# Attention into top-1 expert layers on one Trainium2 core: rows of 528 floats in place of 576, with the partial logits copied to a tile of their own

## The chip, the core and the metric

The kernel runs on one core of one Trainium2 chip, in one launch. Its time is the device time in microseconds (us); the figure shown is the median of three runs. An "execution" below is one such run; one further execution was taken with the hardware profiler, and all rows below come from that one.

## The reference

For each of 8 batches and 8 heads, 576 tokens are compressed into 32 memory slots (a softmax of `phi` over the tokens gives the weights `a`), each query attends over those 32 slots, and the heads are put side by side as the input `x` (4608 tokens of 512) of a layer with 8 experts, of which each token uses one.

```
a = softmax(phi over seq);  k_m = a^T k;  v_m = a^T v           # 32 slots per head
x = softmax(q k_m^T / sqrt(64)) v_m                             # heads side by side: [4608, 512]
logits = x @ w_gate;  e = argmax(logits)
gate = softmax(logits)[e] * sigmoid(x @ w_output_gate)[e]
out = gate * (relu(x @ w1[e]) @ w2[e])
```

## The kernel before

Work goes by pairs of batches (`bp`, four of them, 1152 tokens each). `memories` makes the slots of a pair. `attention` runs 20 steps, five to a pair; the order of the parts inside a step is written out by hand (`ORDER`, line 37): score matmuls (`scores`, L846), transposition and subtraction of the maximum (`shift`), exponential (`expo`), division, transposition back, and then the value matmuls `values` (L892) twice for a step, for two chunks of 128 tokens (one chunk in a pair's fifth step).

The operand of the value matmuls holds, for each group of two heads, 128 columns of values and 16 more columns: the slots' values already multiplied by the two gate matrices. So for each token the product has four quarters of 144 = `XQ` floats: 128 of `x`, and 16 partial sums of the 8 logits and the 8 output-gate logits. It lies in two banks of PSUM, two quarters in each. `values` copies the whole of it, 128x576, with one instruction of ScalarE (ACT) to the tile `xo` (L904); `store` (L1008) writes `xo` to the DRAM table `xs`, whose rows are `XROW` = 576 floats, and eight parts later a reduction on VectorE (DVE, L1021) adds up the four partial sums out of `xo` into `lg`. PSUM has two buffers of such banks (one in the joint stage below); scores and values take turns in them. The tile `xo` has two buffers.

When a pair is done, `rank` (L906) picks the expert of each token and its gate, writes the gate over the 16 partial sums of each row's first quarter (`gt`, L980 to 985), and works out lists of rows by expert (`route_early`, `route_late`). The DMA queue of SyncE (SP) issues loads, stores and the gate writes in program order; GpSimd (POOL) issues the gathers. `gather` (L524) fetches 128 rows of `xs` for a tile: the first five groups as whole rows (L537), the rest as quarters of a row, one indirect DMA for each quarter (L531). `turn_x` (L1052) turns the gathered rows so that features lie on partitions, and `several` and `single` run the two expert products, with each fp32 weight split into two parts.

From step 17 of 20 on, attention is interleaved with the expert work by hooks between the matmuls (the joint stage); before that, TensorE has only attention to do.

Of the kernel before, what the change touches and what calls it, by code (L numbers as in the profile page):

```python
# [17 lines left out]
P = 128  # L18
# [39 lines left out]
LAST = 1  # L58
WHOLE = tuple(range(NPE))
XQ = 144  # L60
XROW = 4 * XQ


HEADS = (0, 2, 4, 6, 1, 3, 5, 7)
# [3 lines left out]
def attention_moe(tc, phiT, kv, qT, wgo, wall, out):  # L68
# [3 lines left out]
    with contextlib.ExitStack() as ctx:  # L72
# [451 lines left out]
        def gather(z):  # L524
            z["xg"] = xgs.tile()
            for k in range(z["nb"]):
                q = z["q0"] + k
                if z["quart"]:
                    rows = 4 * z["rows"]
                    for b in range(quarters(z, k)):  # L530
                        G.indirect_dma_start(  # L531
                            out=z["xg"][:, k, XQ * b:XQ * b + XQ], out_offset=None,
                            in_=xs[0:z["rows"]].rearrange("t (a q) -> (t a) q", a=4),
                            in_offset=bass.IndirectOffsetOnAxis(ap=z["idx"][2][:, b, q:q + 1], axis=0),
                            bounds_check=rows - 1, oob_is_err=False)
                    continue
                G.indirect_dma_start(  # L537
                    out=z["xg"][:, k], out_offset=None, in_=xs[0:z["rows"]],
                    in_offset=bass.IndirectOffsetOnAxis(ap=z["idx"][0][:, q:q + 1], axis=0),
                    bounds_check=z["rows"] - 1, oob_is_err=False)  # L540
# [348 lines left out]
            V.transpose(z["aT"][:, 0:n * M].rearrange("p (a m) -> p a m", m=M), z["ea"][:, 0:n, 0:M])  # L889
            tick()  # L890

        def values(bp, c, z, xo):  # L892

            px = banks()
            for g in range(2):
                sl = slice(XQ * g, XQ * g + XQ)
                for b in (c // 4,) if c < 8 else (0, 1):
                    o, n = (256 * g + (c % 2) * P, P) if c < 8 else (128 * g + 64 * b, 64)
                    to = 0 if c < 8 else 64 * b
                    for r in range(2):  # L900
                        h = slice(64 * r, 64 * r + 64)
                        T.matmul(px[to:to + n, r, sl], z["aT"][h, o:o + n], ves[2 * bp + b][h, g],  # L902
                                 start=True, stop=True)
            A.copy(xo[:, c % 2], px[:, :, 0:2 * XQ])  # L904

        def rank(bp, lg):  # L906

# [13 lines left out]
            rki = rt.tile([P, NCH], I32, name="rki")  # L921
            ri = rt.tile([P, NCH], I32, name="ri")
            row = rt.tile([P, NCH], F32, name="row")
            gt = rt.tile([P, NCH, XQ - P], F32, name="gt")
            oh = ohg[:, cs]
            dscb = desc[:].unsqueeze(1).to_broadcast(b3)
            lmb = lm[:].unsqueeze(2).to_broadcast(b3)
# [22 lines left out]
            def rest():  # L950
                yield from take_pr()
                yield from hold(LATE["pe"])

                pr = ps_r.tile([P, NCH, E], F32, name="pr")
                T.matmul(pr[:], strict[:], oh, start=True, stop=False)
                if bp:
                    T.matmul(pr[:], ones_b[:], ohcs[bp - 1][:].unsqueeze(1).to_broadcast(b3), start=False, stop=False)
                for c in range(1, NCH):
                    T.matmul(pr[:, c:], ones_b[:], oh[:, 0:NCH - c], start=False, stop=(c == NCH - 1))
                yield  # L960
                V.tensor_reduce(gd[:], w2_[:], axis=AX.X, op=ALU.add)
                A.activation(zs[:], zs[:], AF.Exp, scale=-1.0)
                yield
                yield from hold(LATE["dve"])
                V.tensor_tensor(w1_[:], oh, pr[:], ALU.mult)
                taken.clear()
                V.tensor_scalar(gd[:], gd[:], 1e-9, None, ALU.add)
                yield
                with nc.allow_low_precision("whole numbers"):
                    V.tensor_reduce(rki[:], w1_[:], axis=AX.X, op=ALU.add)  # L970
                V.tensor_scalar(zs[:], zs[:], 1.0, None, ALU.add)
                yield
                V.tensor_scalar(ri[:], rki[:], 127, None, ALU.bitwise_and)
                V.tensor_scalar(jg[:, cs], rki[:], 7, None, ALU.arith_shift_right)
                V.tensor_tensor(gd[:], gd[:], zs[:], ALU.mult)
                yield
                V.tensor_copy(row[:], ri[:])  # L977
                V.reciprocal(gd[:], gd[:])
                yield
                V.tensor_copy(gt[:], gd[:].unsqueeze(2).to_broadcast([P, NCH, XQ - P]))  # L980
                for b in range(2):
                    nc.sync.dma_start(
                        xs[t0 + b * S:t0 + b * S + 512, P:XQ].rearrange("(c p) d -> p c d", p=P),
                        gt[:, 4 * b:4 * b + 4])
                    nc.sync.dma_start(xs[t0 + b * S + 512:t0 + b * S + 576, P:XQ], gt[64 * b:64 * b + 64, 8])
                for c in range(NCH):
                    (G if AWP else V).tensor_scalar(  # L987
                        Aw[:, bp * NCH + c], iota_row[:], row[:, c:c + 1], None, ALU.is_equal)
                    if c % 3 == 2:
                        yield  # L990
                ranked.append(bp)
# [13 lines left out]
                        gens.remove(g)  # L1005
                yield

        def store(bp, c2, xo, lg):  # L1008
            t0 = bp * 2 * S
            b, n = c2 // 2, 2 if c2 < 4 else 1  # L1010
            if c2 < 4:
                r = t0 + b * S + (c2 % 2) * 256
                nc.sync.dma_start(xs[r:r + 256].rearrange("(c p) d -> p c d", p=P),
                                  xo[:].rearrange("p c r d -> p c (r d)"))
            else:
                for b_ in range(2):
                    nc.sync.dma_start(
                        xs[t0 + b_ * S + 512:t0 + b_ * S + 576],
                        xo[64 * b_:64 * b_ + 64, 0].rearrange("p r d -> p (r d)"))
            xl = xo[:].rearrange("p c r (g d) -> p c (r g) d", g=2)[:, 0:n, :, P:XQ]  # L1020
            defer("lg", lambda: V.tensor_reduce(  # L1021
                lg[:, 2 * c2:2 * c2 + n], xl.rearrange("p c q l -> p c l q"), axis=AX.X, op=ALU.add))

        def last(g):
            r = None
# [26 lines left out]
        def turn_x(z, c):  # L1052
# [4 lines left out]
            if c == 0:  # L1057
                z["x"] = (mo.tile([P, 4, 3 * P], F32R, name="xh"),
                          None if nb == 2 else mo.tile([P, 4, 3 * P], F32R, name="xl"))
                if z["quart"]:  # L1060
                    z["xt"] = {}
                    z["g"] = env["xt"].tile([P, 3], F32, name="gx")
                    for b in range(4):
                        k = nb - (nb == 2 and b > 1)
                        A.copy(z["g"][32 * b:32 * b + 32, 0:k], xg[0:32, 0:k, XQ * b + P])
            xh, xl = z["x"]
            if z["quart"]:

# [14 lines left out]
            else:  # L1083
# [1 line left out]
                    return  # L1085
                pt = bank([512], "ps")
                for k in range(nb):
                    T.transpose(pt[:, k * P:(k + 1) * P], xg[:, k, c * XQ:c * XQ + P], ident[:])
                pt = pt[:, 0:n]
            A.copy(xh[:, c, 0:n], pt)  # L1090
            V.tensor_tensor(xl[:, c, 0:n], pt, xh[:, c, 0:n].bitcast(F32), ALU.subtract)
# [21 lines left out]
        def attention():  # L1113
# [8 lines left out]
            for t in range(NT + LAG["V"]):  # L1122
                for w in ORDER:
# [12 lines left out]
                    elif w == "V0" and 0 <= g < NT:  # L1136
# [2 lines left out]
                            mem.step()  # L1139
                        if g == 5 * bp:  # L1140
                            lgs[bp] = rt.tile([P, NCH, 16], F32, name="lg", bufs=2)
                        xo = wk.tile([P, 2, 2, 2 * XQ], F32, name="xo", bufs=2)
                        values(bp, 2 * c, st[g], xo)
                    elif w == "V1" and 0 <= g < NT:
                        if c < 4:
                            values(bp, 2 * c + 1, st[g], xo)
                        store(bp, c, xo, lgs[bp])
                    elif w == "C" and 0 < g < NT:
                        while 2 * (g // 5) + (g % 5 >= 2) not in kTs:
                            mem.step()  # L1150
# [293 lines left out]
```

## Time and profile before

| | |
|---|---|
| median of three runs | 553.86 us (553.79 to 554.71) |
| the profiled execution | 555.65 us, its span 553.9 us |
| TensorE (PE) busy | 509.0 us (92%) |
| VectorE, ScalarE, GpSimd busy | 352.0, 287.9, 232.6 us |
| mean granted clock of TensorE | 0.969 |
| traffic | 123.54 MB, 223 GB/s over the span |

The span runs from the first to the last instruction; 1.75 us of the profiled execution lie outside it. "Granted clock" is the share of full speed that TensorE was given. Busy shares over the whole span mix an attention stage (to about 117 us), in which no engine is busy all the time, with an expert stage, in which TensorE is.

### The profile page before, as it was taken

The numbers are of one execution on the slowest core, as the hardware profiler recorded it, in microseconds if no ns is written. First come the engines' busy times: TensorE is split into PE (matmuls) and PEld (weight loads), VectorE is DVE, ScalarE is ACT, GpSimd is POOL, SyncE is SP. The second block draws the span as 40 slices with busy tenths as digits, with TensorE's granted clock in tenths as the row PEclk, the third lists the DMA queues.
The fourth block names the chain that finished last, engine by engine and source line by source line (L and its number), as shares of the span: only waits on it lengthen the run. The fifth ranks groups of instructions, "written<-read, shape, count | busy, mean of one in ns | idle before, by whom it ended". The sixth has DMA issues, their size and how long they took to land. (4 is left out here: it accounts for less than half of the span.)

```text
span 553.9 us, 10578 instructions
## 1 busy us (share of the span) xinstructions
PE 509.0 (92%) x3859; PEld 437.6 (79%) x3859; DVE 352.0 (64%) x779; ACT 287.9 (52%) x536; POOL 232.6 (42%) x254
## 2 busy tenths in 40 slices
PE   3788877599999999999999999999999999999993
PEld 2455555388689799898998989897999899888982
DVE  4384979957776659996436556944786387549310
ACT  3475765454454446553435546834775377358310
POOL 2242585851434034410466562563447463710101
PEclk9877989979999999999999999999999999999997
DMA  8999999995457756963547574875586577643001
GB/s 310 416 389 392 411 373 400 320 351 175 132 192 240 225 168 222 309 183 115 154 139 259 174 233 126 262 219 182 179 264 177 190 244 241 201 162 98 30 21 43
DMA packets 41998, 123.54 MB, mean 223 GB/s; under 512 B 10256, under 2 KB 10320, under 8 KB 41552
## 3 DMA queue, kind: packets, MB, share of 16 engines
q1 hardware_dynamic: 35136, 102.71, 56.0%
q0 software_dynamic: 6800, 20.06, 10.3%
q8 instruction: 32, 0.52, 0.4%
q14 instruction: 30, 0.25, 0.1%
HBM read 102.40 MB, written 20.35 MB: 222 GB/s over the span
## 5 line engine op out<-in xcount | busy, mean ns | idle before, releaser
L1275 PE MATMUL bps<-whl,hh 128*128 128x512 f32 x640 | 193.6, 394 | 0.9 <-issue 0.9
L1238 PE MATMUL bps<-xh,whl 128*128 128x384 f32 x640 | 166.0, 336 | 0.0
L590 DVE TENSOR_TENSOR whl<-w,whl 128x1024 fp32r<-128x1024 f32 x112 | 136.1, 1220 | 11.6 <-ACT whl L576 11.2
L1275 PEld LDWEIGHTS bps<-whl,hh 128*128 128x128 f32 x640 | 119.9, 188 | 26.5 <-issue 2.2
L576 ACT CAST whl<-w 128x1024 fp32r<-128x1024 f32 x112 | 116.4, 1044 | 19.3 <-PE bps L1275 14.9
L1238 PEld LDWEIGHTS bps<-xh,whl 128*128 128x128 f32 x640 | 115.8, 188 | 1.3 <-issue 0.6
L531 POOL DMA_INDIRECT xg<-xs,idx_ql x84 | 98.2, 1168 | 25.6 <-issue 23.8
L1238 PE MATMUL bps<-xl,whl 128*128 128x384 f32 x320 | 107.0, 334 | 0.0
L1275 PE MATMUL bps<-whl,hl 128*128 128x512 f32 x240 | 93.8, 391 | 0.5 <-issue 0.5
L1243 DVE SCALAR_TENSOR_TENSOR hl<-bps,hh 128x384 fp32r<-128x384 f32 x80 | 43.9, 554 | 69.9 <-ACT hh L1242 48.1
L1242 ACT ACTIVATE hh<-bps 128x384 fp32r<-128x384 f32 x80 | 38.9, 492 | 85.2 <-PE bps L1238 70.8
L1211 POOL DMA_INDIRECT out<-y,idx_ol x23 | 25.0, 1089 | 113.3 <-ACT y L1210 54.2
L1238 PEld LDWEIGHTS bps<-xl,whl 128*128 128x128 f32 x320 | 60.1, 188 | 0.3
L1275 PEld LDWEIGHTS bps<-whl,hl 128*128 128x128 f32 x240 | 45.1, 188 | 9.1 <-issue 0.8
L871 POOL TENSOR_TENSOR ea<-ea,mx 128x512 f32<-128x512 f32 (+1 forms) x20 | 19.3, 967 | 46.8 <-DVE mx L869 42.4
L1233 PE MATMUL bps<-xh,whl 128*128 128x384 f32 x128 | 37.7, 338 | 0.0
L1234 PE MATMUL bps<-xh,whl 128*128 128x256 f32 x128 | 35.7, 279 | 0.0
L904 ACT COPY xo<-bpd 128x576 f32<-128x576 f32 x36 | 22.6, 639 | 20.6 <-PE bpd L902 11.9
L1210 ACT ACTIVATE y<-bps,gx 128x512 f32<-128x512 f32 x19 | 13.1, 687 | 36.8 <-PE bps L1275 30.1
L1211 POOL DMA_INDIRECT out<-y,idx_ob x9 | 10.0, 1112 | 48.8 <-ACT y L1210 38.0
L902 PE MATMUL bpd<-ve_b,aT 64*128 64x144 f32 (+1 forms) x320 | 27.8, 321 | 3.0 <-DVE ea L865 3.0
L987 POOL TENSOR_SCALAR Aw<-iota_row,row 128x128 bf16<-128x128 bf16 x36 | 25.8, 735 | 8.9 <-DVE row L977 8.9
(263 smaller groups left out, 586.8 us busy)
## 6 DMA issues: line engine op xcount, KB each, us to landing
w<-wall SPq DMA_DIRECT2D x112, 512.0 KB
kvt<-kv SPq DMA_DIRECT2D x32, 512.0 KB
xs<-xo SPq DMA_DIRECT2D x16, 576.0 KB
qt<-qT SPq DMA_DIRECT2D x16, 512.0 KB
ph<-phiT SPq DMA_DIRECT2D x3, 1152.0 KB
kv<-kv SPq DMA_DIRECT2D x4, 512.0 KB
xg<-xs,idx_ql POOLq DMA_INDIRECT x84
ph<-phiT SPq DMA_DIRECT2D x4, 288.0 KB
```

The source lines that it names most:

```text
L531: G.indirect_dma_start(out=z["xg"][:, k, XQ * b:XQ * b + XQ], out_offset=None, in_=xs[0:z["rows"]].rearrange("t (a q) -> (t a) q", a=4), i ...
L576: A.copy(hl[:, 0], w[:])
L590: V.tensor_tensor(hl[:, 1], w[:], hl[:, 0].bitcast(F32), ALU.subtract)
L902: T.matmul(px[to:to + n, r, sl], z["aT"][h, o:o + n], ves[2 * bp + b][h, g], start=True, stop=True)
L987: (G if AWP else V).tensor_scalar(Aw[:, bp * NCH + c], iota_row[:], row[:, c:c + 1], None, ALU.is_equal)
L1211: G.indirect_dma_start(out=out, out_offset=bass.IndirectOffsetOnAxis(ap=z["idx"][1][0:n, z["q0"] + k:z["q0"] + k + 1], axis=0), in_=y[0:n] ...
L1233: T.matmul(pb, w[:, 0, o:o + P], x[0][:, cc], start=(cc == 0), stop=False)
L1234: T.matmul(pb[:, 0:256], w[:, 1, o:o + P], x[0][:, cc, 0:256], start=False, stop=(cc == 3))
L1238: T.matmul(pb, w[:, b, o:o + P], x[a][:, cc, 0:n_], start=(n == 0), stop=(n == 11))
L1242: A.activation(h_[:, j], pb, AF.Relu)
L1243: V.scalar_tensor_tensor(l_[:, j], pb, 0.0, h_[:, j].bitcast(F32), ALU.max, ALU.subtract)
L1275: T.matmul(py[k], a, w[:, b, DM * f:DM * f + DM], start=(u == 4 and f == 0 and n == 0), stop=(u == 7 and f == 1 and n == len(ps) - 1))
```

## The change

Rows of `xs` go from 4x144 to 4x132 floats: 128 values of each quarter and 4 more. The copy from PSUM to `xo` takes those 132 columns of each quarter (528 elements), and a second copy takes the 16 partial sums of each quarter (64 elements) to a new tile `xl` of two buffers, from which the reduction now reads. The first 4 of the 16 partial sums are still stored, and the gate is written over them (4 floats a row in place of 16). Counts of DMAs, gathers and matmuls stay.

```diff
-XROW = 4 * XQ
+XR = 132
+XROW = 4 * XR
...
                         G.indirect_dma_start(
-                            out=z["xg"][:, k, XQ * b:XQ * b + XQ], out_offset=None,
+                            out=z["xg"][:, k, XR * b:XR * b + XR], out_offset=None,
...
-        def values(bp, c, z, xo):
+        def values(bp, c, z, xo, xl):
...
-            A.copy(xo[:, c % 2], px[:, :, 0:2 * XQ])
+            pv = px[:, :, 0:2 * XQ].rearrange("p r (g d) -> p r g d", g=2)
+            A.copy(xo[:, c % 2], pv[:, :, :, 0:XR])
+            A.copy(xl[:, c % 2], pv[:, :, :, P:XQ])
...
-            gt = rt.tile([P, NCH, XQ - P], F32, name="gt")
+            gt = rt.tile([P, NCH, XR - P], F32, name="gt")
...
-                V.tensor_copy(gt[:], gd[:].unsqueeze(2).to_broadcast([P, NCH, XQ - P]))
+                V.tensor_copy(gt[:], gd[:].unsqueeze(2).to_broadcast([P, NCH, XR - P]))
                 for b in range(2):
                     nc.sync.dma_start(
-                        xs[t0 + b * S:t0 + b * S + 512, P:XQ].rearrange("(c p) d -> p c d", p=P),
+                        xs[t0 + b * S:t0 + b * S + 512, P:XR].rearrange("(c p) d -> p c d", p=P),
                         gt[:, 4 * b:4 * b + 4])
-                    nc.sync.dma_start(xs[t0 + b * S + 512:t0 + b * S + 576, P:XQ], gt[64 * b:64 * b + 64, 8])
+                    nc.sync.dma_start(xs[t0 + b * S + 512:t0 + b * S + 576, P:XR], gt[64 * b:64 * b + 64, 8])
...
-        def store(bp, c2, xo, lg):
+        def store(bp, c2, xo, xl, lg):
...
-            xl = xo[:].rearrange("p c r (g d) -> p c (r g) d", g=2)[:, 0:n, :, P:XQ]
+            lv = xl[:].rearrange("p c r g d -> p c (r g) d")[:, 0:n]
             defer("lg", lambda: V.tensor_reduce(
-                lg[:, 2 * c2:2 * c2 + n], xl.rearrange("p c q l -> p c l q"), axis=AX.X, op=ALU.add))
+                lg[:, 2 * c2:2 * c2 + n], lv.rearrange("p c q l -> p c l q"), axis=AX.X, op=ALU.add))
...
-                        A.copy(z["g"][32 * b:32 * b + 32, 0:k], xg[0:32, 0:k, XQ * b + P])
+                        A.copy(z["g"][32 * b:32 * b + 32, 0:k], xg[0:32, 0:k, XR * b + P])
...
-                    T.transpose(pt[:, k * P:(k + 1) * P], xg[:, k, c * XQ:c * XQ + P], ident[:])
+                    T.transpose(pt[:, k * P:(k + 1) * P], xg[:, k, c * XR:c * XR + P], ident[:])
...
-                        xo = wk.tile([P, 2, 2, 2 * XQ], F32, name="xo", bufs=2)
-                        values(bp, 2 * c, st[g], xo)
+                        xo = wk.tile([P, 2, 2, 2, XR], F32, name="xo", bufs=2)
+                        xl = wk.tile([P, 2, 2, 2, XQ - P], F32, name="xl", bufs=2)
+                        values(bp, 2 * c, st[g], xo, xl)
```

## Rows read from the trace of the kernel before

**Rows 1.** Busy time by stretch of the span: start and end, its length, then for PE, its weight loads (PEld), DVE, ACT and POOL the busy us (and instructions), the granted clock of TensorE, the busy share of the 16 DMA engines and the GB/s that they moved.

```profile
20.00:50.00 30.00, 21.84 (x392) 13.39 (x386) 18.07 (x37) 16.64 (x40) 10.92 (x14) 0.75 1.02 393
50.00:79.70 29.70, 24.74 (x466) 16.74 (x464) 23.83 (x66) 19.72 (x46) 18.22 (x27) 0.91 1.03 407
79.70:86.30 6.60, 5.56 (x101) 3.94 (x105) 4.64 (x13) 5.74 (x14) 4.06 (x6) 1.00 1.01 342
86.30:103.00 16.70, 12.27 (x276) 8.61 (x265) 15.39 (x66) 7.05 (x16) 11.39 (x17) 1.00 0.98 355
103.00:117.00 14.00, 9.11 (x121) 6.72 (x119) 10.42 (x22) 8.09 (x16) 8.71 (x9) 0.76 1.02 384
117.00:545.90 428.90, 425.42 (x2380) 381.28 (x2378) 272.16 (x545) 221.85 (x387) 174.03 (x160) 1.00 0.59 184
```

**Rows 2.** Who waited for whom: the waiting engine, tile and line, then what ended the wait; us in total, times, the longest. The first two rows are of the whole span, the last three of the stretch up to 117 us.

```profile
PEld pk L764 <- DMA kvt<-kv: 5.1, 4, 2.0
PE pk L764 <- DMA kvt<-kv: 3.9, 4, 1.8
...
PEld bpd L855 <- ACT xo L904: 0.9, 3, 0.3
DVE lg L1021 <- ACT xo L904: 0.8, 1, 0.8
PE bpd L855 <- ACT xo L904: 0.5, 2, 0.2
```

**Rows 3.** Order of time on TensorE: start, us, instruction, count, and in brackets the idle time before it and what ended it.

```profile
44.87 0.82 PE L764 MATMUL pk<-kvt,at 128*32 128x128 f32 x16 [0.61 <-DMA kvt<-kv]
...
62.75 0.64 PE L764 MATMUL pk<-kvt,at 128*32 128x128 f32 x16 [0.44 <-DMA kvt<-kv]
...
80.61 1.25 PE L902 MATMUL bpd<-ve_b,aT 64*128 64x144 f32 x16
...
82.35 0.67 PE L855 MATMUL bpd<-qt,kT 64*32 64x256 f32 x16 [0.25 <-ACT xo L904]
...
110.55 0.74 PE L790 MATMUL bpa<-ident,kvm 128*128 128x128 f32 x2 [4.08 <-ACT kvm L781]
111.22 2.29 PE L902 MATMUL bpd<-ve_b,aT 64*128 64x144 f32 x16
```

**Rows 4.** The same for ScalarE, around 60 us and from 79 to 86 us.

```profile
60.31 0.64 ACT L904 COPY xo<-bpd 128x576 f32<-128x576 f32 x1 [1.00 <-DVE aT L889]
...
81.27 0.37 ACT L796 COPY vT_b<-bpa 64x256 f32<-64x256 f32 x1
81.66 1.18 ACT L904 COPY xo<-bpd 128x576 f32<-128x576 f32 x2
82.73 0.65 ACT L875 ACTIVATE ea<-ea 128x512 f32<-128x512 f32 x1
83.42 0.37 ACT L741 COPY a<-bpa 64x256 f32<-64x256 f32 x1
83.80 0.37 ACT L742 COPY a<-bpa 64x256 f32<-64x256 f32 x1
84.19 1.31 ACT L745 COPY at<-bpa 128x512 f32<-128x512 f32 x2
85.62 0.64 ACT L904 COPY xo<-bpd 128x576 f32<-128x576 f32 x1
```

**Rows 5.** The same for VectorE.

```profile
60.98 0.26 DVE L1021 TENSOR_REDUCE lg<-xo 128x16 f32<-128x64 f32 x1 [0.78 <-ACT xo L904]
...
86.30 0.27 DVE L1021 TENSOR_REDUCE lg<-xo 128x16 f32<-128x64 f32 x1
...
102.68 0.17 DVE L247 TENSOR_SCALAR idx_ga<-iv 128x6 int32<-128x6 f32 x1
```

**Rows 6.** The same for GpSimd.

```profile
104.00 1.25 POOL L537 DMA_INDIRECT xg<-xs,idx_ga  x1 [1.38 <-DVE ea L865]
105.56 1.00 POOL L537 DMA_INDIRECT xg<-xs,idx_ga  x1 [0.30 <-DVE ve_b L809]
106.86 1.54 POOL L537 DMA_INDIRECT xg<-xs,idx_ga  x1 [0.31 <-issue]
108.43 1.14 POOL L871 TENSOR_TENSOR ea<-ea,mx 128x512 f32<-128x512 f32 x1
```

**Rows 7.** Groups of instructions by line: count, busy us and mean ns of one, then the idle time before them and what ended it.

```profile
L904 ACT COPY xo<-bpd 128x576 f32<-128x576 f32 x36 | 22.6, 639 | 20.6 <-PE bpd L902 11.9 <-issue 7.3 <-DVE aT L889 1.0
L745 ACT COPY at<-bpa 128x512 f32<-128x512 f32 x16 | 9.4, 586 | 8.0 <-PE bpa L735 7.6
L1245 ACT COPY hl<-bps 128x192 f32<-128x192 f32 x32 | 8.5, 317 | 0.0
L1065 ACT COPY gx<-xg 32x3 f32<-32x3 f32 (+2 forms) x36 | 6.8, 190 | 0.7
L809 DVE COPY ve_b<-bpa 128x32 f32<-128x32 f32 x8 | 1.3, 164 | 3.4 <-PE bpa L804 3.4
L980 DVE COPY gt<-gd 128x144 f32<-128x144 f32 x4 | 1.2, 294 | 0.0
```

**Rows 8.** The copy of line 904 alone by stretch: length, ACT busy us (and instructions), granted clock, DMA share, GB/s.

```profile
0.00:117.00 117.00, 16.16 (x26) 0.88 1.00 378
117.00:190.00 73.00, 6.42 (x10) 1.00 0.65 208
```

More of the change, by code (lines that the diff above doesn't have):

```diff
@@ L1013, in store @@
                 nc.sync.dma_start(xs[r:r + 256].rearrange("(c p) d -> p c d", p=P),
-                                  xo[:].rearrange("p c r d -> p c (r d)"))
+                                  xo[:].rearrange("p c r g d -> p c (r g d)"))
             else:
@@ L1018, in store @@
                         xs[t0 + b_ * S + 512:t0 + b_ * S + 576],
-                        xo[64 * b_:64 * b_ + 64, 0].rearrange("p r d -> p (r d)"))
-            xl = xo[:].rearrange("p c r (g d) -> p c (r g) d", g=2)[:, 0:n, :, P:XQ]
+                        xo[64 * b_:64 * b_ + 64, 0].rearrange("p r g d -> p (r g d)"))
+            lv = xl[:].rearrange("p c r g d -> p c (r g) d")[:, 0:n]
             defer("lg", lambda: V.tensor_reduce(
-                lg[:, 2 * c2:2 * c2 + n], xl.rearrange("p c q l -> p c l q"), axis=AX.X, op=ALU.add))
+                lg[:, 2 * c2:2 * c2 + n], lv.rearrange("p c q l -> p c l q"), axis=AX.X, op=ALU.add))
         def last(g):
@@ L1141, in attention @@
                             lgs[bp] = rt.tile([P, NCH, 16], F32, name="lg", bufs=2)
-                        xo = wk.tile([P, 2, 2, 2 * XQ], F32, name="xo", bufs=2)
-                        values(bp, 2 * c, st[g], xo)
+                        xo = wk.tile([P, 2, 2, 2, XR], F32, name="xo", bufs=2)
+                        xl = wk.tile([P, 2, 2, 2, XQ - P], F32, name="xl", bufs=2)
+                        values(bp, 2 * c, st[g], xo, xl)
                     elif w == "V1" and 0 <= g < NT:
                         if c < 4:
-                            values(bp, 2 * c + 1, st[g], xo)
-                        store(bp, c, xo, lgs[bp])
+                            values(bp, 2 * c + 1, st[g], xo, xl)
+                        store(bp, c, xo, xl, lgs[bp])
                     elif w == "C" and 0 < g < NT:
```

## The prediction, made before the changed kernel ran

> **What bounds the kernel now.** I read the busy times by stretch first, then the waits, then the order of time on each engine, and last the groups of instructions for prices.
>
> By stretch [rows 1] the span falls in two. From 117 us on TensorE is busy 425.42 of 428.90 us at full clock: whatever another engine or a transfer gains there has 3.5 us of idle time, all of TensorE's pauses together, to be found in. Before 117 us TensorE is busy about three quarters of the time, the DMA engines are busy for all of it (a share of 0.98 to 1.03), and ScalarE and VectorE take turns in being the fullest: VectorE has 15.39 of 16.70 us from 86.3 to 103 us, ScalarE 5.74 of 6.60 us from 79.7 to 86.3 us. So the question is what sets the pace before 117 us, and the busy share alone would say the transfers.
>
> The waits say otherwise [rows 2]. TensorE waited for a load of `kvt` in four places, 3.9 us, and the last of those is at 62.75 us [rows 3]; after it no matmul of attention waits for a transfer, though the DMA engines stay full. They are full because loads run ahead as far as buffers let them. Read backwards from the first expert matmul, the chain is one of engines in their program order:
> - TensorE stood still for 4.08 us before 110.55 us for ScalarE's `kvm`, which came behind an exponential, which waited for a subtraction on GpSimd, which stood behind three gathers issued from 104.00 us on [rows 3, 6].
> - Those need the list that VectorE ended at 102.85 us, at the end of a stretch in which it hardly paused since 86.30 us [rows 1, 5].
> - That stretch begins with the reduction of the partial logits at 86.30 us, which follows the copy at 85.62 us (it ends at 86.26 us), which ends a run of ScalarE that is nearly without a gap from 79.7 us on [rows 4, 5].
> - One pair of batches earlier, VectorE waited 0.78 us at 60.98 us for the same copy of the same chunk, the one at 60.31 us [rows 4, 5].
> - Before that the chain passes the loads that TensorE waited for at 44.87 us [rows 3].
>
> So ScalarE's copies of line 904 lie on the path in a few known places, and transfers in one.
>
> **The second copy.** Each of the 36 copies becomes two. The slope between 512 and 576 elements is (639 - 586) / 64 = 0.83 ns per element, so the one of 528 takes 639 - 48 x 0.83 = 599 ns, 0.04 us less [rows 7]. No row shows a copy of 64 elements on 128 partitions. Its nearest rows are 190 ns (32x3) and 317 ns (128x192); on the line between them it is 190 + 61 x 127 / 189 = 231 ns [rows 7]. Two copies of 0.64 us in a row take 1.18 us, so the second starts 0.54 us after the first, 0.10 us before the first has ended [rows 4]. Whether a short copy that reads the same banks starts early too isn't shown. If both starts overlap, a pair adds 0.19 - 0.10 - 0.04 = 0.05 us to ScalarE's queue; if the short one has no overlap, 0.231 - 0.04 = 0.19 us. I take the middle, 0.12 us. On ScalarE that is 36 x 0.12 = 4.3 us in all, 26 of the pairs before 117 us [rows 8], and nearly all of it falls into pauses, since line 904 itself comes after 20.6 us of idle time [rows 7].
>
> On the path are four of them. (1) At 60.31 us: the reduction now waits for the second copy, since the chunk's partial sums are in the new tile: +0.12 us. (2) and (3) The pair at 81.66 us: what is queued behind it on ScalarE is the exponential of 82.73 us, the copies of `a` and of `at`, and through them the value matmuls whose copy is the one at 85.62 us; TensorE waits too, since the scores at 82.35 us need the bank that the first of the pair reads [rows 3, 4]: +0.24 us. (4) The copy at 85.62 us, ahead of the reduction at 86.30 us: +0.12 us. Together +0.48 us, between 0.20 and 0.76.
>
> The other 22 before 117 us cost nothing as long as ScalarE reaches them with idle time ahead; the waits of TensorE for `xo` there are 0.5 us in 2 places [rows 2]. From 117 us on ten pairs add 10 x 0.19 = 1.9 us at most to 221.85 us in 428.90 [rows 1, 8]; TensorE's queue of expert matmuls hides that, and if that cover were gone it would be those 1.9 us.
>
> **The stores and the waits around them.** A chunk pair is 256 rows, now 192 bytes shorter: 49 KB less for each store. At the 378 GB/s of the stage [rows 8] that is 0.13 us of all DMA engines. Before the wait at 44.87 us one store is queued ahead of the load that it waits for: -0.13 us. The earlier load of 62.75 us isn't on the path, since VectorE works without a pause from 60.98 us on. The store itself waits for the shorter first copy alone. The tile `xo` is now released by its store alone, and the new tile by the reduction, which runs before the tile's next turn in the trace; I cost both at nothing.
>
> **The gate column.** The copy of `gt` goes from 144 to 36 elements: from 294 ns to about the 164 ns of a copy of 32 [rows 7], -0.13 us, once on the path (the one of the second pair, inside VectorE's full stretch); the first pair's is followed by a wait for scores. The gate write to DRAM keeps its count of pieces, 1152 to a pair of batches, of 16 bytes in place of 64. What that does to its landing isn't shown. The first gather starts 1.15 us after its list is ready, and the page puts that on a transposition that it doesn't read [rows 5, 6]; up to 1.15 us of it may be the landing of the gate column. So this edit is worth between -1.15 us (the small pieces land at once) and +1.15 us (they take as much longer). I take 0, since the count of pieces stays.
>
> **The gathers.** POOL issues as many of them; they move 8.3% fewer bytes beside a TensorE that doesn't pause. Nothing, unless the cover goes. The reduction reads as many elements in another stride: nothing.
>
> A rule speaks against counting bytes here. The rows above give only rates. The Trainium skill, "DMA: Bandwidth & Descriptors", section "How a descriptor splits into AXI transactions", says that a read that doesn't start at a multiple of 256 bytes pays for the bytes from the multiple below it, in beats of 32 bytes. Rows of 2304 bytes all start at one; rows of 2112 bytes start 0, 64, 128 or 192 bytes past one, so by an estimate from that page a whole row falls from 72 beats to a mean of 69, 4.2% and not 8.3%, and a quarter from a mean of 21 to 20.5. No run here shows it. By it a gain by bytes would be about half.
>
> **Sum.** +0.48 - 0.13 - 0.13 = +0.22 us, between -0.06 and +0.50. The profiled execution took 555.65 us, 553.9 us of it the span; the median of the plain runs is 553.86 us, so I put the difference on the median: 554.1 us, with 553.8 to 554.4 as this case's own range.
>
> **The rivals.** (B) The transfers set the pace up to 117 us. Then all the bytes count: by then 26 chunks of 128 rows are stored, 3328 rows x 192 bytes = 0.64 MB, and two pairs' gate columns, 2304 x 48 bytes = 0.11 MB; 0.75 MB at 378 GB/s is 2.0 us, which gives 551.9 us. The full DMA engines speak for it, the missing waits after 62.75 us against it [rows 1 to 3]. By the rule above it would be half, about 552.9 us. (C) The gate column's landing holds the first gather and comes sooner: 554.1 - 1.15 = 552.95 us. (D) Slower: ScalarE's queue is the path at most copies before 117 us, and not at four. Its place is the attention stage, its price 0.05 to 0.19 us for each of 26 pairs; with 0.12 it is 3.1 - 0.26 = +2.9 us, 556.8 us. It decides where ScalarE's idle time ahead of the copies (20.6 us over 36) is not there in the step that matters; the gapless run up to 86 us shows how such a step looks, and busy shares of 55 to 66% elsewhere before 79.7 us speak against it [rows 1, 4, 7]. (E) TensorE's clock. It was granted 0.75 from 20 to 50 us and 0.76 from 103 to 117 us [rows 1], after pauses such as the 4.08 us; the same 16 value matmuls took 2.29 us there against 1.25 us at full clock [rows 3]. A shift of a pause can add or take away one such stretch: about 1 to 1.5 us either way, 552.9 or 555.4 us.
>
> **How the numbers follow.** A measurement of this kernel can tell about 0.2%, 1.1 us. The likeliest case, with its small sum, has 0.56, all within 0.2%. B has 0.13: 0.10 faster, and 0.03 within, since stores that end after the last step that waits for them don't count. C has 0.05, faster in 0.04. D has 0.14, slower in 0.13. E has 0.12, split evenly, and faster or slower in 0.10. So faster 0.19, same 0.63, slower 0.18. The range goes from 552.0 to 555.9 us: it leaves out most of D and the far half of B, and holds the gate column's two ends.
>
> **What would show it.** If I am right, 36 copies of about 600 ns stand beside 36 of 190 to 231 ns; the reduction at the start of `rank` comes 0.1 to 0.5 us later for the second pair; the DMA share before 117 us stays at about 1.0 with fewer GB; and the first expert matmul stands where it stood, within half a us. B is right if the waits of TensorE for `kvt` shrink and the whole stage is shorter by 1 to 2 us. C is right if the first gather starts sooner after its list. D is right if TensorE's waits for ScalarE, 0.5 us for `xo` now, grow by microseconds. E shows as another granted clock in one of the stretches. A difference that arises after 117 us would be against all of this.

## The result, and the profile of the changed kernel

The changed kernel takes 557.43 us (median of ten runs, 556.58 to 558.65), the kernel before 554.00 us in ten runs on the same chip; the ratio is 1.0051 [1.0036, 1.0067]. By the ratio it is slower by some 2.8 us (the medians differ by 3.4 us), and its median is above the range that was given (552.0 to 555.9). The profiled execution took 557.53 us, 1.9 us more than that of before.

The page gives the total and the engines' busy time; DVE, ACT and POOL lie within 3.2 us of what they were, and TensorE has 4.0 us more:

```profile
span 555.8 us, 10620 instructions
PE 513.0 (92%) x3859; PEld 439.7 (79%) x3859; DVE 351.9 (63%) x779; ACT 291.1 (52%) x572; POOL 234.9 (42%) x254
```

The same stretches as [rows 1], with the same columns:

```profile
50.00:79.70 29.70, 24.95 (x468) 17.09 (x466) 23.89 (x66) 20.23 (x56) 18.18 (x26) 0.91 1.02 389
79.70:86.30 6.60, 5.59 (x60) 3.62 (x60) 4.19 (x12) 4.96 (x14) 3.69 (x5) 0.74 1.01 268
86.30:103.00 16.70, 12.80 (x283) 9.03 (x282) 14.63 (x64) 8.60 (x23) 11.39 (x19) 1.00 0.97 352
103.00:117.00 14.00, 9.12 (x143) 6.53 (x139) 10.92 (x22) 7.90 (x19) 9.54 (x9) 0.76 0.99 358
117.00:547.00 430.00, 428.71 (x2384) 383.28 (x2382) 272.99 (x547) 223.02 (x398) 176.21 (x160) 1.00 0.59 182
```

The reader is to see two things. From 79.7 to 86.3 us the granted clock is 0.74 where it was 1.00. And in the last row TensorE is busy for 428.71 us at full clock with 2384 matmuls, where it was busy for 425.42 us with 2380: about the same number of matmuls at the same clock took some 3 us longer.

The waits up to 120 us, as in [rows 2]:

```profile
PEld pk L765 <- DMA kvt<-kv: 3.9, 4, 1.9
...
PE pk L765 <- DMA kvt<-kv: 3.1, 4, 1.6
...
DVE lg L1024 <- ACT xl L907: 1.4, 2, 0.8
...
PEld bpd L856 <- ACT xl L907: 1.1, 3, 0.4
```

They are as before within 1.2 us each; only the releaser is now the second copy. TensorE's order of time, as in [rows 3], the last row being the first expert matmul (it stood at 117.08 us):

```profile
82.72 1.11 PE L856 MATMUL bpd<-qt,kT 64*32 64x256 f32 x16 [0.32 <-ACT xl L907]
83.77 2.61 PE L736 MATMUL bpa<-ident,ph 128*128 128x128 f32 x10
...
112.17 2.29 PE L903 MATMUL bpd<-ve_b,aT 64*128 64x144 f32 x16
...
118.03 0.44 PE L1242 MATMUL bps<-xh,whl 128*128 128x384 f32 x1 [0.26 <-DVE xl L1094]
```

The scores at 82.72 us take 1.11 us for the 16 that took 0.67 us: this is the stretch at half clock. ScalarE, as in [rows 4]:

```profile
60.38 0.60 ACT L906 COPY xo<-bpd 128x528 f32<-128x528 f32 x1 [0.58 <-DMA xs<-xo]
60.87 0.22 ACT L907 COPY xl<-bpd 128x64 f32<-128x64 f32 x1
...
81.96 0.60 ACT L906 COPY xo<-bpd 128x528 f32<-128x528 f32 x1
82.45 0.22 ACT L907 COPY xl<-bpd 128x64 f32<-128x64 f32 x1
82.56 0.62 ACT L906 COPY xo<-bpd 128x528 f32<-128x528 f32 x1
83.05 0.24 ACT L907 COPY xl<-bpd 128x64 f32<-128x64 f32 x1
83.15 0.66 ACT L876 ACTIVATE ea<-ea 128x512 f32<-128x512 f32 x1
```

Each instruction starts about 0.1 us before the one ahead of it has ended, and the second copy does so too: 0.49 us after the first, and the next one 0.11 us after it. A pair so takes 0.60 us from start to start (81.96 to 82.56), where one copy of 576 took 0.54. The groups by line, as in [rows 7]:

```profile
L906 ACT COPY xo<-bpd 128x528 f32<-128x528 f32 x36 | 21.6, 601 | 20.0 <-PE bpd L903 11.9 <-issue 7.3 <-DMA xs<-xo 0.6
L907 ACT COPY xl<-bpd 128x64 f32<-128x64 f32 x36 | 8.0, 221 | 0.0
...
L1279 PE MATMUL bps<-whl,hh 128*128 128x512 f32 x640 | 195.2, 397 | 0.0
```

The copies came out as costed. The last row is the surprise: the same group of the kernel before, line 1275 there, reads

```profile
L1275 PE MATMUL bps<-whl,hh 128*128 128x512 f32 x640 | 193.6, 394 | 0.9 <-issue 0.9
```

640 matmuls that the change doesn't touch take 3 ns more each. Matmuls overlap, so what counts is the time from the start of one to the start of the next, taken here and below as differences of the start times in the trace. For a matmul of 512 columns its mean rose from 227.6 ns to 231.1 ns, and for one of 384 columns from 173.6 to 175.0 ns (in the second half of the stage, where no matmul waits for its operands). From the first to the last expert matmul it is 428.81 us, where the profiled execution of before has 427.42 us. In that one four matmuls, at 379 to 381 and 485 us, start 0.70 to 0.92 us after the one ahead in place of 0.23; these pauses are 2.2 us in all, and the trace puts them on "issue". Without them the stage is some 3.5 us longer after the change.

### The profile page after: what moved, and what is told of

It is laid out like the page before. It is cut to its first block, busy times and chain, and to the rows that moved or that the text cites. A ratio compares the mean times of both kernels' runs of the same rounds, so it can differ in the third digit from the quotient of the medians.

```text
span 555.8 us, 10620 instructions
## 1 busy us (share of the span) xinstructions
PE 513.0 (92%) x3859; PEld 439.7 (79%) x3859; DVE 351.9 (63%) x779; ACT 291.1 (52%) x572; POOL 234.9 (42%) x254
## 5 line engine op out<-in xcount | busy, mean ns | idle before, releaser
L906 ACT COPY xo<-bpd 128x528 f32<-128x528 f32 x36 | 21.6, 601 | 20.0 <-PE bpd L903 11.9
L866 DVE STREAM_TRANSPOSE ea<-bpd 128x512 f32<-128x512 f32 (+1 forms) x20 | 13.2, 659 | 26.4 <-PE bpd L856 18.4
```

The lines of the kernel that those rows point to most:

```text
L906: A.copy(xo[:, c % 2], pv[:, :, :, 0:XR])
```

## The experiments

Three theories were put up. One, the place: smaller tiles let all tiles behind them in SBUF (the on-chip memory that tiles lie in) move, and TensorE's pace depends on where the operands of the expert matmuls lie. The rivals: the second copy costs ScalarE more than was worked out, or the rows, gathers and stores of the new length do (their transfers would then disturb TensorE). The addresses are those of the built programs. In each partition `gt` takes 160 bytes in place of 576 (144 of them used) and each of three gather tiles `xg` 576 bytes less. What matters, as it turned out, is what a tile's byte address in its partition leaves after division by 256, its remainder:

| remainder by 256 | before | after |
|---|---|---|
| split weights `whl`, first two tiles | 96 | 192 |
| `whl`, next two tiles | 96 | 128 |
| `whl`, last six tiles | 96 | 0 |
| `xh`, `xl`, `hh`, `hl` | 96 | 128 |

Before, all agreed. After, only two of the ten weight tiles agree with the other operand. Each of the four sets of runs below had runs of the kernel before on the same chip; ratios are against those. "Pace" is the mean start-to-start time of the matmuls of 512 columns in groups where a product is made of three matmuls of the split parts (`whl` with `hh`, `hl` and `hh` again), counted where no matmul waits for its operands; "expert stage" goes from the first to the last expert matmul; both are from one profiled execution.

**1. The old places, with the rest of the change** (e1_place). `gt` and `xg` are allocated at their old size and used in part.

```diff
-        xgs = Ring([P, 3, XROW], F32, "xg")
+        xgs = Ring([P, 3 * 4 * XQ], F32, "xg")
...
-            gt = rt.tile([P, NCH, XR - P], F32, name="gt")
+            gt = rt.tile([P, NCH * (XQ - P)], F32, name="gt")
...
```

> The changed kernel, but its gate tile and its gather tiles take as much SBUF as before (the surplus is unused), so that the weight tiles, the gathered rows and the expert operands stand at the addresses of the kernel before; the gather's partition pitch inside a tile stays 528. Theory 1 (of the 1.9 us in the profiles, 0.95 arise before the first expert matmul, by the second copy and a further stretch at half clock near 83 us, and the rest in the expert stage, where matmuls take 1 to 2% longer because their operands stand at other SBUF addresses): the first half stays and the second goes, some 555 to 555.3 us where before has 554.0 and changed 557.4; the median of the expert matmuls of 512 columns goes back from a start-to-start of 232 ns to 227 ns. Rival (the slower matmuls come from the smaller gathers or from chance): no change against the changed kernel, 557.4 us.

554.32 us, ratio 0.9995 [0.9979, 1.0011]; pace 227.5 ns, expert stage 424.90 us. The whole loss is gone with the copies, the rows and the gathers left as in the changed kernel. Only places in SBUF differ. The expectation's other half, that some 1 us ahead of the expert stage would stay, did not come.

**2. All tiles moved alike** (e2_shift). The kernel before with an unused tile of 32 bytes ahead, so that all remainders are 128.

```diff
+        rt.tile([P, 8], F32, name="shift", bufs=1)
```

> The kernel before with one unused tile of 32 bytes, which moves the weight tiles, the gathered rows and the expert operands from addresses that leave 32 after division by 64 to multiples of 64, as they stand in the changed kernel; nothing else. Theory 1: slower than before by 1 to 2.5 us (555 to 556.5 us), all of it after 117 us, with expert matmuls of 512 columns at 230 ns or more from start to start; the granted clock near 83 us stays at full. Rival: 554.0 us, as before.

554.99 us, 1.0013 [0.9999, 1.0027]; pace 227.5 ns. What this run was to show, that addresses at multiples of 64 bytes are slow in themselves, fell.

**3. The second copy alone** (e3_copy, and g3_copy later on another chip). The kernel before with rows of 576; each copy is split in two that write the same tile.

```diff
-            A.copy(xo[:, c % 2], px[:, :, 0:2 * XQ])
...
+            A.copy(ov[:, :, :, 0:132], pv[:, :, :, 0:132])
+            A.copy(ov[:, :, :, P:XQ], pv[:, :, :, P:XQ])
```

> The kernel before with ScalarE's copy split as in the changed kernel, into one of 132 columns of each quarter and one of the 16 partial sums, both into the old tile; rows, gathers, gate column and all addresses as before. Theory 1: the attention stage is longer by 0.4 to 1.0 us (with the half-clock stretch near 83 us if the four copies on the path are what brings it), the expert stage is that of before: 554.4 to 555 us. Rival (the shorter rows cause the attention stage's loss, by other landing times): 554.0 us and no half-clock stretch near 83 us.

> The kernel before with the split copy alone a second time. By the prediction's sum for the copies alone +0.48 us (ratio 1.0009); from the five-fold copy, which cost 12.6 us for 104 further copies in the attention stage, one further copy to a pair would be up to 3 us (1.005) if the cost were in proportion, and less if ScalarE's pauses take up the first.

555.52 us, 1.0015 [0.9998, 1.0032], and 555.34 us, 1.0018 [0.9997, 1.0038]; pace 227.5 ns in both. Taken together (weighted by their intervals) this is +0.16% with half an interval of 0.13%, about 0.9 us: barely told from nothing, and less than the 0.51 to 0.74% that the changed kernel lost in its three sets of runs. It is also a larger dose than the change's. Here both copies write columns 128 to 131 of each quarter, and the second starts 0.63 us after the first (35.51 and 36.14 us in e3), so that a pair takes 0.74 us from start to start: 0.20 us more than one copy of 576, where the change adds 0.06.

**4. The short rows alone** (e4_rows). The copy is whole again, into a tile of 576; stores pick 132 of each 144 floats out of it, two DMAs to a pair of chunks and pieces of 528 bytes.

```diff
...
+                for k in range(2):
+                    nc.sync.dma_start(xs[...].rearrange("p (q d) -> p q d", q=4),
+                                      xo[:, k].rearrange("p r (g d) -> p (r g) d", g=2)[:, :, 0:XR])
...
```

> Rows of 528 floats without a second copy: the old tile of 576 floats is stored without 12 of the 16 partial sums of each quarter, in pieces of 528 bytes and with two DMAs in place of one for each pair of chunks; addresses as before. Theory 1: the rows by themselves are worth nothing that shows, 553.6 to 554.4 us. Rival B of the prediction (the transfers set the pace): 552 to 553 us. If the small pieces or the extra DMA issues cost, 554.5 to 556 us, with SyncE's queue later before 117 us.

567.85 us, 1.0236 [1.0211, 1.0260]; first expert matmul at 131.53 us, expert stage 425.63 us, pace 227.5 ns. It loses 13 us, all of it before the expert stage, and the waits up to 135 us name the stores:

```profile
ACT xo L905 <- DMA xs<-xo: 14.8, 5, 4.6
PE pk L765 <- DMA kvt<-kv: 6.9, 6, 2.4
```

ScalarE waited for `xo` to be stored in five places, up to 4.6 us, which it hardly did in the changed kernel (0.6 us in all). So this run measures the stores, in small pieces and with twice as many DMAs, and not the rows; the rows can't be had alone in this way. Its expert stage says that gathers of short rows don't slow TensorE.

**5. Both kernels again, and the weights moved against the rest** (r2_after, r1_before, e5_after_off32, e7_before_256). The first two are the two kernels unchanged. The others put an unused tile ahead of the six last weight tiles, which moves those and one tile of raw weights that no matmul reads: 32 bytes on the changed kernel (their remainder goes from 0 to 32, so they no longer start at multiples of 8192), 160 bytes on the kernel before (from 96 to 0).

```diff
+            env["gap"] = ctx.enter_context(tc.tile_pool(name="gap", bufs=1))
+            env["gap"].tile([P, 8], F32, name="gap")    # 40 on the kernel before
```

> The changed kernel once more, for a second profile beside the kernels of this call. If the slower expert matmuls belong to the kernel (to where its tiles stand), they are there again: 231 ns from start to start for 512 columns outside the first three groups, against 227 ns, and an expert stage of some 428.8 us from its first to its last matmul. If they were chance, 227 ns and 425 us. The start of the first expert matmul shows how far the attention stage varies by itself (118.03 us the first time).

> The kernel before once more, for a second profile. Expert matmuls of 512 columns at 227 ns again; its five long gaps between expert matmuls at 379 to 486 us, 2.2 us beyond the usual spacing, are gone if they are chance. The start of the first expert matmul (117.08 us the first time, 118.46 to 120.51 us in the kernels with small edits) shows whether the attention stage alone varies by 1 to 3 us; if it does, the 0.95 us between the two first profiles can't be put down to the second copy by single profiles.

> The changed kernel with an unused tile of 32 bytes taken at the point where the six late tiles of the split weights are allocated, which moves those six and one tile of raw weights by 32 bytes (from multiples of 8192 to 32 bytes past one) and nothing else. Theory 1a (it is those six tiles, at such round addresses, that the matmuls read more slowly): 227 ns again, an expert stage of 425 us, and the time of the kernel before within 0.15%. Rival (another moved tile, such as the gathered rows or the hidden activations, or the smaller rows): 231 ns, 428.8 us, as slow as the changed kernel.

> The kernel before with an unused tile of 160 bytes at the same point, which moves its six late weight tiles to multiples of 256 that are no multiples of 512, and nothing else. If a multiple of 256 is enough, expert matmuls of 512 columns take 231 ns and the time is 0.4 to 0.7% above before. If it takes a rounder address, 227 ns and no change.

| | us | ratio | pace, ns | expert stage, us |
|---|---|---|---|---|
| r1_before | 553.96 | 0.9994 [0.9972, 1.0015] | 227.5 | 425.35 |
| r2_after | 558.62 | 1.0074 [1.0046, 1.0101] | 231.1 | 428.85 |
| e5_after_off32 | 559.00 | 1.0085 [1.0057, 1.0113] | 231.7 | 429.63 |
| e7_before_256 | 560.13 | 1.0086 [1.0057, 1.0114] | 231.3 | 429.21 |

The loss is found again. e5 is against the thought that multiples of 8192 are what hurts. e7 is the strongest of these runs: the kernel before, with nothing but 160 unused bytes in SBUF, loses as much as the changed kernel. Its row of the 640 matmuls:

```profile
L1275 PE MATMUL bps<-whl,hh 128*128 128x512 f32 x640 | 195.4, 397 | 0.0
```

e2 and e7 together say that the difference between the tiles counts, not where they are. Nor is it another engine at work on the moved tiles: of the matmuls of 512 columns that stream one of the six tiles in e7, 85 of 445 have no instruction of VectorE, ScalarE or GpSimd under way from 0.5 us before their start to the start of the next, and their median is 234 ns, as for the other 360.

**6. Agreement made and broken through the gather tile** (f1_after_256 and, on another chip, the same kernel as g2_after_256 beside the unchanged one, g1_after; f3_before_64). 64 unused bytes in each gather tile bring all remainders of the changed kernel to 192; on the kernel before they spread them to 96, 160 and 32.

```diff
-        xgs = Ring([P, 3, XROW], F32, "xg")
+        xgs = Ring([P, 3 * XROW + 16], F32, "xg")
...
```

> The changed kernel with 64 unused bytes more in each gather tile (6400 bytes in place of 6336), so that the weight tiles, the gathered operands and the hidden activations all leave the same remainder by 256 again (192), as in the kernel before (96 for all). Theory 1b (a matmul is slower when the addresses of its streamed operand and of the weights that are loaded beside it differ by something that is no multiple of 256; the absolute address doesn't matter): 227 ns from start to start for 512 columns, an expert stage of 425 us, and the time of the kernel before within 0.2%, some 4 us under the changed kernel. Rival (the shorter gathers or some other tile): 231 ns, 428.8 us, 558 us.

> The kernel before with the same 64 unused bytes in each gather tile, which takes the remainders by 256 apart (early weight tiles 96, the next two and the operands 160, the six late ones 32). Theory 1b: slower than before by 0.5 to 0.9%, all of it in an expert stage of 428.5 to 430 us; 231 ns or more where the late tiles are streamed. Rival: no change, 554.5 us.

> The changed kernel a third time, beside the next two on one chip. Theory: slower than before by 0.5 to 0.8%, with 231 to 232 ns from start to start for expert matmuls of 512 columns and an expert stage of 428.5 us or more.

> The changed kernel with 64 unused bytes in each gather tile a second time. Theory 1b: 227 ns and 0.6% under the changed kernel. Against before it measures what the second copy and the shorter rows are worth together with the addresses out of the way: by the prediction's sum +0.22 us (ratio 1.0004); if ScalarE's copies are on the path more often than at four places, 1.001 to 1.003; if the shorter rows gain more than the copies cost, below 0.999.

f1: 560.47 us, 0.9990 [0.9956, 1.0023], pace 227.6 ns, expert stage 427.60 us, of which 2.6 us are four pauses as in the first profile of before. f3: 561.11 us, 1.0033 [1.0003, 1.0062], pace 231.6 ns, expert stage 430.27 us with one such pause of 0.9 us. On that chip single runs of one kernel lie 5 to 13 us apart (the kernel before from 555.23 to 568.14 us), so these ratios say little, and f3's is under the 0.5 to 0.9% that was expected; the paces are clear. On a quieter chip g1 took 558.51 us, 1.0066 [1.0044, 1.0088], and g2 553.87 us, 0.9989 [0.9970, 1.0009]; expert stage 428.69 and 424.98 us. Between g1 and g2 lie 64 unused bytes in each gather tile and 4.6 us of the median, 3.7 us of them in the expert stage. Summed over the start-to-start times, the matmuls of 512 columns gave 2.7 us of it, those of 384 columns 0.8, those of 256 columns 0.1.

The trace of g1 shows the pace change as the tile changes. TensorE's order of time in one group of the second expert product (a row of x2 holds two matmuls):

```profile
299.84 0.39 PE L1279 MATMUL bps<-whl,hl 128*128 128x512 f32 x1
300.07 0.61 PE L1279 MATMUL bps<-whl,hh 128*128 128x512 f32 x2
300.52 0.39 PE L1279 MATMUL bps<-whl,hl 128*128 128x512 f32 x1
300.75 0.61 PE L1279 MATMUL bps<-whl,hh 128*128 128x512 f32 x2
301.20 0.39 PE L1279 MATMUL bps<-whl,hl 128*128 128x512 f32 x1
301.43 0.62 PE L1279 MATMUL bps<-whl,hh 128*128 128x512 f32 x2
301.89 0.39 PE L1279 MATMUL bps<-whl,hl 128*128 128x512 f32 x1
302.11 0.63 PE L1279 MATMUL bps<-whl,hh 128*128 128x512 f32 x2
302.58 0.40 PE L1279 MATMUL bps<-whl,hl 128*128 128x512 f32 x1
302.81 0.63 PE L1279 MATMUL bps<-whl,hh 128*128 128x512 f32 x2
303.28 0.39 PE L1279 MATMUL bps<-whl,hl 128*128 128x512 f32 x1
```

From one row of `hl` to the next are three matmuls: 299.84, 300.52, 301.20 are 0.68 us apart (227 ns each), 301.89, 302.58, 303.28 are 0.69 to 0.70 us apart (about 232 ns each). From 301.65 us on the streamed weight tile is one with remainder 0; up to then it was one with 128, which agrees with `hh` and `hl`. The same stretch of g2 keeps 0.68 us throughout:

```profile
300.11 0.39 PE L1279 MATMUL bps<-whl,hl 128*128 128x512 f32 x1
...
300.79 0.39 PE L1279 MATMUL bps<-whl,hl 128*128 128x512 f32 x1
...
302.15 0.39 PE L1279 MATMUL bps<-whl,hl 128*128 128x512 f32 x1
...
302.83 0.39 PE L1279 MATMUL bps<-whl,hl 128*128 128x512 f32 x1
...
303.51 0.39 PE L1279 MATMUL bps<-whl,hl 128*128 128x512 f32 x1
```

**7. A difference of the other sign** (f4_before_224). As e7 with 224 unused bytes, so that the six tiles lie 32 below the rest.

> The kernel before with 224 unused bytes ahead of the six late weight tiles, whose remainder by 256 becomes 64 while the operands stay at 96. How the pace goes with the difference: so far a streamed weight tile 64, 128 and 160 bytes past the operand's remainder gave 230, 232.5 and 234 ns, and a stationary one 64 bytes past the streamed operand's gave no loss. If the loss grows with the difference taken upward (here 224), 234 ns or more; if the distance counts in both directions (here 32), 228 to 230 ns and 0.1 to 0.4% above before.

563.33 us, 1.0030 [0.9994, 1.0066], on the same unquiet chip; pace 230.8 ns as a mean, and 233 ns where one of the six tiles is streamed; expert stage 432.20 us, of which 4.0 us are five pauses. A difference of 32 bytes downwards is not small in its cost, and 224 upwards is no slower than 160: neither branch of the expectation came as it stands.

**8. Five small copies for one** (f5_copies5). e3 with the small copy done five times, the same values each time.

```diff
...
+            for _ in range(5):
+                A.copy(ov[:, :, :, P:XQ], pv[:, :, :, P:XQ])
```

> The kernel before with the split copy, its small copy issued five times in place of once (the same 64 elements to the same place); rows and addresses as before. It multiplies the second copy's cost. By the prediction's sum (four pairs on the path, 0.1 to 0.2 us for each small copy) four further ones cost 1.6 to 3.2 us in the attention stage beyond the split copy's own, with an expert stage of 425 us: 556.5 to 559 us. By rival D (26 pairs on the path) it is 10 to 20 us. If ScalarE's pauses hide them all, 555 us.

578.43 us, 1.0325 [1.0267, 1.0383]; first expert matmul at 131.69 us, 12.6 us later than in e3, pace 227.6 ns, expert stage 432.24 us where 425 was expected. Of its 7.3 us beyond e3, 2.4 us arise in the first 400 expert matmuls, beside which the ten later pairs lie, and most of the rest in five pauses on "issue". The four places of the prediction's sum gave 1.6 to 3.2 us for this run and fell; it came as by rival D (10 to 20 us). ScalarE's order of time and the waits up to 131 us:

```profile
34.95 0.60 ACT L906 COPY xo<-bpd 128x528 f32<-128x528 f32 x1 [0.23 <-PE bpd L902]
35.58 1.19 ACT L908 COPY xo<-bpd 128x64 f32<-128x64 f32 x5
```

```profile
DVE lg L1025 <- ACT xo L908: 5.5, 2, 2.7
PEld bpd L855 <- ACT xo L908: 4.3, 7, 1.5
```

Small copies to one and the same tile follow each other by (1.19 - 0.213) / 4 = 0.24 us, so four more add 0.98 us to a pair. 12.6 us are 13 such doses, so at this dose it is as if half of the 26 pairs before the expert stage lay on the path. At the dose of the change itself, 0.06 us, this puts the copies' cost, by estimate, between 4 and 13 x 0.06, that is 0.2 to 0.8 us.

## Why the prediction was wrong

**The step that failed** is the one that took TensorE's own time from 117 us on for fixed: "From 117 us on TensorE is busy 425.42 of 428.90 us at full clock". The prediction asked what other engines and transfers could put into that stage ("Nothing, unless the cover goes") and gave TensorE's pace no term in the sum, without a reason. The runs showed 3.7 us there (g1 against g2). Shorter rows make `gt` and `xg` smaller, all that is stacked behind them in SBUF moves by different amounts, and a matmul of 512 columns whose streamed operand lies at another remainder by 256 than the weights loaded beside it takes 2 to 7 ns longer; there are 880 of these, and 1088 of 384 columns that lose up to 2 ns. The experiments show this from both sides: the loss goes when the remainders are made equal (e1, f1, g2) and comes to the kernel before when they are made unequal (e7).

The cover itself held. "TensorE's queue of expert matmuls hides that" was said of the ten later pairs of copies, and the first 400 expert matmuls, beside which they lie, take 93.47 us in the changed kernel where they took 93.42 us. The loss arises after these, when no copy of the change is left. The text names what would refute it, "A difference that arises after 117 us would be against all of this", and there it arose. It could have been seen in the diff, which says which tiles shrink, but no row of the trace of before has more than one alignment, so its price could not be read there.

**What the change does beside that** is close to the sum of +0.22 us. With remainders equal, the changed kernel stands at 0.9995, 0.9990 and 0.9989, together -0.08% with half an interval of 0.12%: -0.4 us, level with the kernel before. The second copy in e3's form is +0.9 us with half an interval of 0.7, for a dose of 0.20 us: 1 to 8 doses, which at the change's 0.06 us are 0.1 to 0.5 us. What the short rows give back would then be some 0.7 us, with half an interval as large, and isn't shown; e4 couldn't measure it.

**Point by point.**
- The second copy: predicted 599 and 231 ns, measured 601 and 221 (the 190 ns that the line to 231 starts from is the mean of three shapes, so it was a rough one). Of its two bounds the lower one is right: both starts overlap, 0.06 us to a pair and not 0.12.
- The reduction at the start of `rank`: predicted later by 0.1 to 0.5 us; for the second pair it starts at 87.91 us where it started at 86.30, but that has the half clock from 82.8 us in it. The one of the first pair, at 61.12 us for 60.98, shows what the copy does: 0.14 us.
- The first expert matmul, predicted within half a us of where it stood: 0.95 us later, which single profiles can't tell from nothing (see E).
- The DMA share stayed at 0.99 before 117 us with 367 GB/s for 378, as predicted. B, by which transfers set the pace, would have shortened the stage; waits for `kvt` shrank by 0.8 us and 1.2 us at most, and no gain is seen.
- C, the gate column: the first gather starts at 105.14 us after 1.54 us of idle time, where it was 1.38 us. It doesn't come sooner.
- D, ScalarE as the path at most copies: at e3's dose of 0.20 us all 26 would be 5.2 us, and 0.9 was measured, so it is not so there; at the dose of f5 the cost is that of 13, and four was too few. How many it is at the dose of the change wasn't measured: four cost 0.24 us and 26 cost 1.6 us.
- E, the clock, did come: a granted 0.74 from 79.7 to 86.3 us. But it is no property of the change: the profiled executions of e7, f3 and f4, which copy as the kernel before does, have a stretch at half clock there too, at 81.7 to 82.1 us. The row of that stretch in e7, with the columns of [rows 1], has the same 0.74:

```profile
79.70:86.30 6.60, 4.48 (x56) 3.31 (x56) 2.78 (x9) 3.99 (x10) 4.31 (x6) 0.74 1.03 336
```

  And over 15 profiled executions (all but e4 and f5) the first expert matmul stands at 116.1 to 121.3 us in the six without a split copy (mean 119.1) and at 118.0 to 120.5 us in the nine with one (mean 119.0). Two executions of one kernel lie up to 1.5 us apart (118.03 and 119.54 us for the changed one). So the 0.95 us between the first two profiles is no more than executions differ by.

For whether a shorter row loses to the rule on 256-byte starts that the prediction cites from the Trainium skill ("DMA: Bandwidth & Descriptors", "How a descriptor splits into AXI transactions"), no run here separates 4% from 8%.

**What stays open.** Which part of the chip makes the remainders matter; the runs show the effect alone. Nor do they show which weights the streamed operand has to agree with, those loaded beside it or those of its own matmul: `xh`, `xl`, `hh` and `hl` share one remainder in every kernel here, so for 512 columns the two are the same. Each difference between 0 and 256 was seen only in the combinations that the tiles gave. And a version faster than the kernel before by more than a run can tell was not found: g2 at 0.9989 [0.9970, 1.0009] is level.

## What to carry to other kernels

A change of a tile's size is a change of every address behind it: where TensorE sets the time, compare the addresses of streamed operands and weights before and after, and look at the start-to-start time of matmuls that the change doesn't touch. If an edit far from the matmuls changes their pace, pad the tile back to its old size and run both; here 64 unused bytes in each of three tiles were worth 4.6 us of the median. And before an early stage is blamed, profile the same kernel twice: the end of the attention stage moved by up to 1.5 us between executions of one kernel here.

## What the runs showed of the hardware

The pace of a matmul in fp32 parts by the remainder of (address of the streamed operand - address of the weights of the next matmul, loaded beside it; for 512 columns those of its own matmul leave the same) by 256, over the expert matmuls of nine profiled executions at full clock; medians of start-to-start times, with their number:

| difference by 256 | 0 | 64 | 128 | 160 | 192 | 224 |
|---|---|---|---|---|---|---|
| 512 columns, ns | 227 (4090) | 229 (524) | 232 (1334) | 234 (890) | 233 (178) | 233 (444) |

For 384 columns of `xl` (here the lower part of the split `x`) it is 173 ns at 0, 64 and 192, and 175 ns at 32, 96 and 128. In the kernel before, the differences are 0, 256, 512 and so on up to 1792 by 2048, all at 227 ns, while 64 and 128 are slow; in the changed kernel 64, 128 and these plus multiples of 256 up to 2048 give 229 to 232 ns: the pattern repeats by 256 bytes. The address itself doesn't count: with all remainders at 96, 128 or 192 the pace is 227 ns.

ScalarE starts a copy about 0.1 us before the one ahead has ended if the two write no element in common (0.49 us after a copy of 0.60 to another tile, 0.54 us after one of 0.64 to the other half of `xo`); where they share elements the second starts after the first has ended (0.63 us after 0.60 in e3, 0.24 us after 0.213 in f5). Stores out of SBUF in pieces of 528 bytes, with two DMAs in place of one, cost the attention stage some 13 us against whole rows. And matmuls of the expert stage that start 0.6 to 1.4 us after the one ahead, for no reason that the trace names but "issue", are in some executions of a kernel and not in others: the first profile of before has four, that of r1 has none of them, and the changed kernel with equal remainders has four in f1 (2.6 us) and none in g2.
